# Last heads reordered, the masked bank stored by column, gneg on ScalarE, the output cast in two halves, and w3 split 6:4 over the partition halves by GpSimd transfers

## The chip, the cores and the metric

The kernel runs on one core of one Trainium2 chip. The metric is the device time of one execution in microseconds, and less is better. Three runs of the kernel before give a median of 532.45 us (530.86 to 533.08).

## What is computed

It is one decode step of a transformer block with attention and a gated feed-forward network side by side: four sequences, one new token each, 32 heads of 192 dimensions, a window of 2048 cached positions, everything in bfloat16.

```python
W = min(4096, max(256, Sk // 4))                 # Sk = 8192, so 2048
xn = _layernorm(x)                               # x: (4, 1, 640)
q = (xn @ wq) ...                                # (4, 32, 1, 192)
k, v = k_cache[:, :, Sk-W:], v_cache[:, :, Sk-W:]
p = softmax(q . k * Dh ** -0.5)
attn = (p . v) @ wo                              # wo: (6144, 640)
ffn = (silu(xn @ w1) * (xn @ w3)) @ w2           # F = 1536
out = x + attn + ffn                             # (4, 1, 640)
```

Each head needs 3 MB of K and 3 MB of V (4 sequences x 2048 rows x 192 x 2 bytes each), so 32 heads read 201 MB. wq (7.9 MB), wo (7.9 MB), w1, w3 and w2 (2.0 MB each) make it 223 MB in all.

## The kernel before, in words

The partitions of a K or V tile are (position block, sequence): partition 4p + b holds 64 consecutive positions of sequence b, 24 KB in one piece. One DMA brings the whole tile of a head. There are two K buffers (`KBUFS`) and three V buffers (`VBUFS`).

A head's scores are made in four quarters, called units; unit u is quarter u % 4 of head u // 4, and there are NU = 128 of them.

- `mult(u)` (L231, VectorE) multiplies a quarter of the K tile with the query into `pr`.
- `adder(u)` (L242, TensorE) adds the 192 products down to 32 columns with six matmuls against the identity.
- `reduce_quarter(u)` (L250, VectorE) adds these 32 columns into the scores `sc`.
- The softmax chain of head h: `chain_lmax` (L254, VectorE, maximum per partition), `chain_tr` (L259, a TensorE transpose), `chain_gmax` (L264 the maximum per sequence, L267 `gneg`, that maximum times -1/sqrt(192); both VectorE), `chain_bc` (L272 a matmul that spreads `gneg`, then ScalarE: L275 `negm` and L278 the exponential `ex`), `chain_z` (L286, VectorE, the weights `z`, put into the columns of their sequence).
- `pv(h)` (L295, 24 matmuls) multiplies `z` with the V tile into a PSUM bank, `o_banks[h % 2]`, of 8 groups (j) x 64 columns.
- `pv_diag(h)` (VectorE) masks that bank into `o_m` (L303), then adds it over j into `o_sb` (L306).
- `ge_sum(h)` (L322, TensorE), `ge_tot` (L311), `ge_rec` (L317), `ge_turn` (L326 `og`, L328 `oT`) and `ge_proj` (matmuls through L212) finish a group of four heads: sum over partitions, division by the softmax sum, turn, and product with the group's rows of `wo` into the accumulator `acc`.

The feed-forward part is `ffn_load` (a whole weight as one DMA on SyncE's queue), `ffn_in` (20 matmuls against `xnT`, L345), `ffn_silu`, `ffn_h` (L352, L355), `w2_load` in three pieces and `ffn_out` (matmuls into `acc`). w1, w3 and w2 take turns in one buffer. At the end L447 casts `acc` to `res`, and two DMAs store its halves (L449 on SyncE, L450 on ScalarE).

The order is written out by hand: nothing is moved by a scheduler. `add(slot, phase, fn, ...)` puts a step into a slot (unit u runs in slot u) at a phase, and the loop at the end issues the steps in that order. Each engine works through its own instructions strictly in this order, so an instruction that waits holds all that come after it on its engine. For the last three heads (H-3, H-2, H-1, below called heads 29, 30 and 31) the table `ends` gives slots of their own:

```python
ends = {H - 3: (NU - 3, NU - 2, NU - 1), H - 2: (NU + 2, NU + 3, NU + 4), H - 1: (NU + 6, NU + 7, NU + 7)}
```

The three numbers are the slots of `pv`, `pv_diag` and `ge_sum`. The last V tiles, w2 and the last two groups of `wo` are all issued around slot NU - 6, in the order V29 (second half), V30, V31 (two halves), w2 (eight of twelve columns), wo of groups 6 and 7, w2 (three columns), w2 (one column).

Of the kernel before, what the change touches and what calls it, by code (L numbers as in the profile page):

```python
# [10 lines left out]
FP32 = mybir.dt.float32  # L11
BF16 = mybir.dt.bfloat16
ALU = mybir.AluOpType
ACTF = mybir.ActivationFunctionType
AX = mybir.AxisListType
# [3 lines left out]
def kernel(  # L19
# [20 lines left out]
    nc = tc.nc  # L40
    P = 128
    B, Sq, D = A_x.shape
    _, H, Sk, Dh = A_k_cache.shape
    W = min(4096, max(256, Sk // 4))
    F = B_w1.shape[1]
    KC = D // P
    FC = F // P
    PB = P // B
    NJ = W // PB
    GQ = 4  # L50
    JQ = NJ // GQ
    NK = Dh // DD
    SCALE = float(Dh) ** -0.5
    EPS = 1e-5
    NG = H // HG
    CT = 32
    QW = HG * Dh
    RPP = QW // P
    NU = H * GQ
    N0 = D // 2  # L60
# [3 lines left out]
    JG = CT // B  # L64
    SW = CT * NI
    SR = NS * CT
# [8 lines left out]
    fpool = ctx.enter_context(tc.tile_pool(name="ffn", bufs=1))  # L75
# [3 lines left out]
    const = ctx.enter_context(tc.tile_pool(name="const", bufs=1))  # L79
    ppool = ctx.enter_context(tc.tile_pool(name="pr", bufs=PBUFS))  # L80
    small = ctx.enter_context(tc.tile_pool(name="small", bufs=3))
# [3 lines left out]
    ps_t = ctx.enter_context(tc.tile_pool(name="ps_t", bufs=1, space=MemoryType.PSUM))  # L85
# [27 lines left out]
    x_sb = const.tile([B, D], BF16, name="x_sb")  # L113
# [3 lines left out]
    for k0 in range(0, KC, 2):  # L117
        n = min(2, KC - k0)
        wt = vpool.tile([P, 2, H * Dh], BF16, tag="vt")
        nc.sync.dma_start(out=wt[:, 0:n, :].rearrange("p k n -> p (k n)"),  # L120
                          in_=wq_v[:, k0:k0 + n, :].rearrange("p k n -> p (k n)"))
# [3 lines left out]
    ffn = {}  # L125

    def ffn_load(name, w):
        wt = fpool.tile([P, KC, F], BF16, tag="w", name=name)
        nc.sync.dma_start(out=wt[:].rearrange("p k n -> p (k n)"), in_=w.rearrange("(p kc) n -> p (kc n)", kc=KC))
        ffn[name] = wt  # L130

    ffn_load("w1", B_w1)

    idb = const.tile([P, P], BF16, name="idb")
# [12 lines left out]
    jmask = const.tile([P, NREP], FP32, name="jmask")  # L147
# [8 lines left out]
                            in1=mask_f[:].unsqueeze(1).to_broadcast([P, NS, B]), op=ALU.mult)  # L156
# [18 lines left out]
    xn = const.tile([B, D], BF16, name="xn")  # L175
# [7 lines left out]
    nc.vector.tensor_copy(out=xnT[:], in_=xnT_ps[:].unsqueeze(2).to_broadcast([P, KC, PB, B]))  # L183

    qbc = const.tile([P, H * Dh], BF16, name="qbc")
    for c0 in range(0, NQ, 6):
        qps = [pool.tile([P, QC], FP32, tag=tag, name="qps")
               for pool, tag in ((ps_add, "ps"), (ps_add, "ps"), (ps_o, "o_ps"), (ps_o, "o_ps"), (ps_m, "mt"), (ps_t, "t"))]
        for kc in range(KC):  # L190
            for i, qp in enumerate(qps):
                nc.tensor.matmul(qp[:], lhsT=xnT[:, kc].rearrange("p a b -> p (a b)"),  # L192
                                 rhs=wq_rows[kc][:, (c0 + i) * QC:(c0 + i + 1) * QC],
                                 start=(kc == 0), stop=(kc == KC - 1))
# [8 lines left out]
    o_banks = []  # L203
# [4 lines left out]
    acc = ps_acc.tile([P, N0], FP32, name="acc")  # L208
    nc.vector.memset(acc[:], 0.0)

    def acc_half(i, lhsT, rhs, first=False, last=False):
        nc.tensor.matmul(acc[i * CT:i * CT + B, :], lhsT=lhsT, rhs=rhs[:, i * N0:(i + 1) * N0], start=first, stop=last)  # L212
# [3 lines left out]
            acc_half(i, lhsT, rhs, last=last)  # L216

    po = ps_po.tile([P, SW + 1], FP32, name="po")
    xr = {}

    def x_load():
        xr["t"] = const.tile([B, D], BF16, name="x_res")
        nc.sync.dma_start(out=xr["t"][:], in_=A_x.rearrange("b s d -> (b s) d"))

    def x_add(i):
        acc_half(i, idb[0:B, 0:B], xr["t"], first=True)

    def mult(u):
        h, g = u // GQ, u % GQ
# [32 lines left out]
    def chain_gmax(h):  # L262
        gmax = small.tile([1, B], FP32, tag="gmax")
        nc.vector.tensor_reduce(out=gmax[:], in_=chs[h][1][0:1, 0:P].rearrange("o (p b) -> o b p", b=B),  # L264
                                axis=AX.X, op=ALU.max)
        gneg = small.tile([1, PB, B], FP32, tag="gneg")
        nc.vector.tensor_scalar_mul(out=gneg[:], in0=gmax[:].unsqueeze(1).to_broadcast([1, PB, B]), scalar1=-SCALE)  # L267
        chs[h].append(gneg)

    def chain_bc(h):  # L270
# [28 lines left out]
            vts.pop(h)  # L299

    def pv_diag(h):
        o_m = small.tile([SR, JG, SW], FP32, tag="o_m", bufs=1, name="o_m")
        nc.vector.tensor_tensor(out=o_m[:], in0=o_banks[h % 2][0:SR], in1=jmask[0:SR].unsqueeze(2).to_broadcast([SR, JG, SW]),  # L303
                                op=ALU.mult)
        o_sb = small.tile([SR, SW], FP32, tag="o_sb", bufs=2, name="o_sb")
        nc.vector.tensor_reduce(out=o_sb[:], in_=o_m[:].rearrange("p j c -> p c j"), axis=AX.X, op=ALU.add)  # L306
        o_sbs[h] = o_sb

    def ge_tot(h):
# [27 lines left out]
    FW = F // HG  # L337
# [3 lines left out]
    def ffn_in(name):  # L341
        ffn["ps"] = ps_t.tile([P, FW], FP32, tag="t", name="f_ps")
        for kc in range(KC):
            for w in range(HG):
                nc.tensor.matmul(ffn["ps"][w * CT:(w + 1) * CT, :], lhsT=xnT[:, kc].rearrange("p a b -> p (a b)")[:, 0:CT],  # L345
                                 rhs=ffn[name][:, kc, w * FW:(w + 1) * FW], start=(kc == 0), stop=(kc == KC - 1))

    def ffn_silu():
        nc.scalar.activation(out=sT[:], in_=ffn.pop("ps")[:], func=ACTF.Silu)

# [22 lines left out]
    def add(slot, phase, fn, *args):  # L373
        sched[slot].append((phase, len(sched[slot]), fn, args))

    ends = {H - 3: (NU - 3, NU - 2, NU - 1), H - 2: (NU + 2, NU + 3, NU + 4), H - 1: (NU + 6, NU + 7, NU + 7)}
    for h in range(H):
        u0, ul = h * GQ, h * GQ + GQ - 1  # L380
        if h >= KBUFS:
            add((h - KBUFS + 1) * GQ, 0, load_k, h)
        if h < H - 3:
            add(u0 + 2, 0, load_v, h)
        elif h == H - 3:
            add(u0 + 2, 0, load_v, h, 0, NJ // 2)
            add(NU - 7, 0, load_v, h, NJ // 2, NJ)
        for u in range(u0, ul + 1):
            add(u, 1, mult, u)
            add(u + 1, 2, adder, u)  # L390
            add(u + 1, 8, reduce_quarter, u)
        add(ul + 1, 9, chain_lmax, h)
        add(ul + 2, 3, chain_tr, h)
        add(ul + 2, 4, chain_gmax, h)
        add(ul + 3, 3, chain_bc, h)
        add(ul + 3, 4, chain_z, h)
        add(ul + 4, 5, ge_tot, h)
        if h % HG == HG - 1:
            add(ul + 4, 9, ge_rec, h // HG)
        v, d, m = ends.get(h, (u0 + L, u0 + L + 1, u0 + L + 2))  # L400
        if h < H - 1:
            add(v, 7, pv, h)
        else:
            add(v - 1, 7, pv, h, 0, NJ // 2)
            add(v, 7, pv, h, NJ // 2, NJ)
        add(d, 8, pv_diag, h)
        add(m, 8, ge_sum, h)
        if h % HG == HG - 1:
            add(m + 1, 0, ge_turn, h // HG)
    e = ends[H - 1][2] + 1  # L410
    for hg in range(NG - 2):
        a = ((hg + 1) * HG - 1) * GQ + L + 4
        add(hg * HG * GQ + 8, 0, wo_load, hg)
# [2 lines left out]
    f = FFN_HEAD * GQ  # L416
    add(5, 7, ffn_in, "w1")
    add(5, 9, ffn_silu)
    add(f, 0, ffn_load, "w3", B_w3)
    add(f + 7, 7, ffn_in, "w3")  # L420
    add(f + 7, 9, ffn_h)
    add(8, 0, x_load)
    add(16, 6, x_add, 0)
    add(17, 6, x_add, 1)

# [5 lines left out]
    add(NU - 6, 0, wo_load, NG - 1)  # L432
    add(NU - 6, 0, w2_load, 1)
    add(NU - 6, 0, w2_load, 2)
    add(e - 1, 7, ffn_out, 0)
    add(e - 1, 8, ge_proj, NG - 2, 0, RPP)
    add(e, 6, ge_proj, NG - 1, 0, RPP)
    add(e, 7, ffn_out, 1)
    add(e, 7, ffn_out, 2)
# [4 lines left out]

    NR = CT + B
    res = ppool.tile([NR, N0], BF16, tag="pr", name="res")
    nc.vector.tensor_copy(out=res[:], in_=acc[0:NR, :])  # L447
    out_v = out.rearrange("b s d -> (b s) d")
    nc.sync.dma_start(out=out_v[:, 0:N0], in_=res[0:B, :])  # L449
    nc.scalar.dma_start(out=out_v[:, N0:D], in_=res[CT:NR, :])  # L450
# [30 lines left out]
```

## Time and profile before

| | |
|---|---|
| median of 3 runs | 532.45 us |
| profiled execution, its own time | 533.66 us |
| its span, first to last instruction | 531.9 us |
| TensorE clock granted, mean | 0.89 |
| busy: TensorE, VectorE, ScalarE, GpSimd | 370.4, 392.5, 29.0, 1.1 us |
| HBM read | 222.96 MB, 419 GB/s over the span |

The profiled execution lies 1.2 us above the median, and 1.8 us of it lie outside the span. The times below are us from the start of the span. In a timeline row the first number is the start, the second how long the row lasted, then come engine, line, operation, `out<-in`, shapes and count; the bracket tells how long the engine stood idle before it and what it waited for. A row with a count can hold several instructions with pauses.

### The profile page before, as it was taken

How to read it: one execution, taken by the hardware profiler on the slowest of the kernel's cores; microseconds unless marked ns; L12 is line 12 of the kernel's file. 1: busy time of each engine (PE TensorE's matmuls, PEld its weight loads, DVE VectorE, ACT ScalarE, POOL GpSimd, SP SyncE). 2: the span in 40 equal slices, each digit the busy share in tenths (PEclk: the TensorE clock that was granted, in tenths of full speed). 3: DMA queues.
4: the chain of work that ended last, by engine and by line, in shares of the span. 5: the costliest groups of instructions: out<-in, count | busy, mean ns of one | idle time of the engine just before them, and what ended most of it. 6: DMA issues, size and time to landing. Idle time of an engine off the chain costs nothing.

```text
span 531.9 us, 4826 instructions
## 1 busy us (share of the span) xinstructions
PE 370.4 (70%) x1986; PEld 143.5 (27%) x1987; DVE 392.5 (74%) x498; ACT 29.0 (5%) x110; POOL 1.1 (0%) x8
## 2 busy tenths in 40 slices
PE   2766567677658776468778676567868776876865
PEld 1322222232213322223222222223222322222323
DVE  3178776788948876887858878788768888878853
ACT  2121000000000000000000000000000000000000
POOL 0000000000000000000000000000000000000000
PEclk9989997979978889998977979899787899799777
DMA  8999999999999999999999999999999999999991
GB/s 359 440 425 432 439 427 427 433 439 421 436 429 440 425 434 426 440 425 436 429 434 429 433 430 435 426 436 433 428 433 436 429 433 434 429 434 422 431 420 48
DMA packets 11861, 223.27 MB, mean 420 GB/s; under 512 B 1328, under 2 KB 1472, under 8 KB 2624
## 3 DMA queue, kind: packets, MB, share of 16 engines
q1 hardware_dynamic: 11824, 222.97, 97.7%
q8 instruction: 15, 0.25, 0.2%
q14 instruction: 6, 0.05, 0.0%
q10 hardware_dynamic: 16, 0.01, 0.0%
HBM read 222.96 MB, written 0.01 MB: 419 GB/s over the span
## 4 chain that ended last, share of the span: by engine, by line
DMA 54%; DVE 34%; PE 10%; issue 1%; ACT 0%; SPq 0%
DMA kt<-in_A_k_cache_dram 50%; DVE pr L231 19%; DVE sc L250 5%; PE ps L242 5%; DMA wt<-in_A_wq_dram 4%; DVE o_sb L306 3%; PE o_ps L295 2%; DVE o_m L303 2%; PE qps L192 1%; DVE z L286 1%; DVE gmax L264 1%; DVE gneg L267 1%; PE acc L212 1%; DVE lmax L254 0%; DVE qbc L198 0%
## 5 line engine op out<-in xcount | busy, mean ns | idle before, releaser
L242 PE MATMUL ps<-pr,idb 128*128 128x512 bf16 x768 | 220.7, 431 | 129.0 <-DVE pr L231 128.7
L231 DVE TENSOR_TENSOR pr<-kt,qbc 128x3072 bf16<-128x3072 bf16 x128 | 223.3, 1745 | 88.4 <-DMA kt<-in_A_k_cache_dram 88.4
L242 PEld LDWEIGHTS <-idb 128*128 128x128 bf16 x768 | 78.7, 105 | 240.5 <-issue 182.3
L295 PE MATMUL o_ps<-vt,z 128*32 128x512 bf16 x768 | 100.1, 531 | 1.4 <-DMA vt<-in_A_v_cache_dram 1.4
L250 DVE TENSOR_REDUCE sc<-ps 128x16 f32<-128x512 f32 x128 | 86.8, 678 | 4.5 <-PE ps L242 4.5
L295 PEld LDWEIGHTS <-z 128*32 128x32 bf16 x768 | 32.0, 109 | 56.9 <-issue 55.1
L306 DVE TENSOR_REDUCE o_sb<-o_m 96x64 f32<-96x512 f32 x32 | 32.4, 1012 | 1.1
L275 ACT COPY negm<-mt 128x1 f32<-128x1 f32 x32 | 5.1, 159 | 449.2 <-PE mt L272 449.2
L303 DVE TENSOR_TENSOR o_m<-o_ps,jmask 96x512 f32<-96x512 f32 x32 | 21.5, 673 | 6.4 <-PE o_ps L295 6.4
L192 PE MATMUL qps<-wt,xnT 128*128 128x512 bf16 x59 | 16.1, 429 | 4.8 <-DMA wt<-in_A_wq_dram 4.8
L322 PE MATMUL po<-o_sb,sel_w 96*32 96x64 f32 x64 | 9.7, 234 | 13.2 <-DVE o_sb L306 11.2
L198 DVE CAST qbc<-qps 128x512 bf16<-128x512 f32 x6 | 3.8, 684 | 17.7 <-PE qps L192 17.7
L286 DVE TENSOR_TENSOR z<-ex,mask_b 128x256 bf16<-128x256 bf16 x32 | 13.1, 411 | 4.9 <-ACT ex L278 4.9
L272 PEld LDWEIGHTS mt<-ones_ff,gneg 1*128 1x128 f32 x64 | 9.6, 186 | 14.1 <-DVE o_m L303 10.6
L272 PE MATMUL mt<-ones_ff,gneg 1*128 1x1 f32 x64 | 12.3, 259 | 0.6 <-DVE gneg L267 0.6
L264 DVE TENSOR_REDUCE gmax<-mt 1x4 f32<-1x128 f32 x32 | 8.8, 274 | 4.8 <-PE mt L259 4.8
L278 ACT ACTIVATE ex<-sc,negm 128x64 bf16<-128x64 f32 x32 | 11.1, 348 | 1.0
L259 PE MATMUL mt<-idf,lmax 128*1 128x128 f32 x32 | 9.6, 298 | 1.1 <-DVE lmax L254 1.1
L192 PEld LDWEIGHTS <-xnT 128*128 128x128 bf16 x60 | 6.4, 107 | 14.1 <-issue 8.2
L311 PEld LDWEIGHTS po<-rsum,tot_w 128*32 128x32 f32 x64 | 5.1, 125 | 18.5 <-issue 18.1
L212 PE MATMUL acc<-wo_t,oT 128*4 128x320 bf16 x96 | 9.6, 318 | 0.0
L322 PEld LDWEIGHTS po<-o_sb,sel_w 96*32 96x32 f32 x64 | 4.4, 109 | 17.0 <-DVE o_sb L306 13.8
(54 smaller groups left out, 66.5 us busy)
## 6 DMA issues: line engine op xcount, KB each, us to landing
kt<-in_A_k_cache_dram SPq DMA_DIRECT2D x32, 3072.0 KB, 18.4
vt<-in_A_v_cache_dram SPq DMA_DIRECT2D x30, 3072.0 KB, 25.7
wo_t<-in_A_wo_dram SPq DMA_DIRECT2D x8, 960.0 KB, 19.7
wt<-in_A_wq_dram SPq DMA_DIRECT2D x2, 3072.0 KB, 13.2
vt<-in_A_v_cache_dram SPq DMA_DIRECT2D x4, 1536.0 KB, 21.1
w<-in_B_w_dram SPq DMA_DIRECT2D x2, 1920.0 KB, 30.0
wt<-in_A_wq_dram SPq DMA_DIRECT2D x1, 1536.0 KB, 19.8
w<-in_B_w_dram SPq DMA_DIRECT2D x1, 1280.0 KB, 29.4
```

The lines of the kernel that those rows point to most:

```text
L192: nc.tensor.matmul(qp[:], lhsT=xnT[:, kc].rearrange("p a b -> p (a b)"), rhs=wq_rows[kc][:, (c0 + i) * QC:(c0 + i + 1) * QC], start=(kc == ...
L212: nc.tensor.matmul(acc[i * CT:i * CT + B, :], lhsT=lhsT, rhs=rhs[:, i * N0:(i + 1) * N0], start=first, stop=last)
L231: nc.vector.tensor_tensor(out=pr[:], in0=kts[h][:, g * JQ:(g + 1) * JQ, :], in1=qbc[:, h * Dh:(h + 1) * Dh].unsqueeze(1).to_broadcast([P, ...
L242: nc.tensor.matmul(ps[:], lhsT=idb[:], rhs=pr[:, :, kk * DD:(kk + 1) * DD], start=(kk == 0), stop=(kk == NK - 1))
L250: nc.vector.tensor_reduce(out=scs[h][:, g * JQ:(g + 1) * JQ], in_=pss.pop(u)[:], axis=AX.X, op=ALU.add)
L264: nc.vector.tensor_reduce(out=gmax[:], in_=chs[h][1][0:1, 0:P].rearrange("o (p b) -> o b p", b=B), axis=AX.X, op=ALU.max)
L272: nc.tensor.matmul(mt[:, P:P + 1], lhsT=gneg[:].rearrange("o p b -> o (p b)"), rhs=ones_ff[0:1, 0:1], start=True, stop=True)
L286: nc.vector.tensor_tensor(out=z[:], in0=ex[:].unsqueeze(2).to_broadcast([P, NJ, B]), in1=mask_b[:].unsqueeze(1).to_broadcast([P, NJ, B]), ...
L295: nc.tensor.matmul(o_ps[s * CT:(s + 1) * CT].rearrange("p j c -> p (j c)"), lhsT=z[:, j:j + JG, :].rearrange("p j b -> p (j b)"), rhs=v[:, ...
L303: nc.vector.tensor_tensor(out=o_m[:], in0=o_banks[h % 2][0:SR], in1=jmask[0:SR].unsqueeze(2).to_broadcast([SR, JG, SW]), op=ALU.mult)
L306: nc.vector.tensor_reduce(out=o_sb[:], in_=o_m[:].rearrange("p j c -> p c j"), axis=AX.X, op=ALU.add)
L322: nc.tensor.matmul(po[sl, 0:SW], lhsT=sel_w[0:SR].rearrange("p a b -> p (a b)"), rhs=o_sbs.pop(h)[:], start=True, stop=True)
```

## The change

**Order of the last heads.** The table `ends` goes. `pv` of head 29 is cut into four quarters in slots NU - 5 to NU - 2. `pv` of head 30 is cut into two halves in slots NU + 1 and NU + 2, that of head 31 into halves in NU + 3 and NU + 4, so that it no longer stands behind `ge_sum` of head 30. `pv_diag` of head 29 moves behind the last scores of head 31. The final turn and projection begin in slot NU + 6 instead of NU + 8.

**Masked bank by (column, j).** `o_m` is stored with j innermost. L303's successor reads the PSUM bank with a step of 64 floats and writes without gaps; L306's successor reads without gaps.

**gneg on ScalarE.** The product with -1/sqrt(192) is a ScalarE instruction.

**Cast in halves.** VectorE casts 160 columns of `acc`, ScalarE the other 160. In the built program ScalarE's half waits for VectorE's half (both write the tile `res`), and both stores wait for ScalarE's.

**x** is added into `acc` from `x_sb`, which is in SBUF already; the second load of x (`x_load`) goes.

**w3.** Partitions 0-63 hold six rows of w3 each and partitions 64-127 four, instead of five everywhere. Four DMAs on GpSimd's queue load 32 partitions each: six rows (18 KB in one piece), four rows (12 KB), six, four. They carry no order against SyncE's queue; the first waits for the reads of w1 in the shared buffer. The left operand for the product, `xsT`, is made in the head of the kernel to fit: eight small VectorE copies of `xn` into `xs`, six TensorE transposes, two VectorE copies. `ffn_in_split` runs 24 matmuls instead of 20.

```diff
+    xs = ppool.tile([B, D], BF16, tag="pr", name="xs")
...
+    for p0, d0, kn in SPLIT:
+        for g in range(HP // CT):
+            v = xn[:, d0 + g * CT * kn:d0 + (g + 1) * CT * kn].rearrange("r (b a k) -> r k a b", a=NA, b=NB)
+            nc.vector.tensor_copy(out=xs_m[:, :, p0 // CT + g], in_=v[:, 0:KM])
+            for k in range(KM, kn):
+                nc.vector.tensor_copy(out=xs_x[:, k - KM, g], in_=v[:, k])
...
-        nc.vector.tensor_scalar_mul(out=gneg[:], in0=gmax[:].unsqueeze(1).to_broadcast([1, PB, B]), scalar1=-SCALE)
+        nc.scalar.mul(out=gneg[:], in_=gmax[:].unsqueeze(1).to_broadcast([1, PB, B]), mul=-SCALE)
...
-        o_m = small.tile([SR, JG, SW], FP32, tag="o_m", bufs=1, name="o_m")
+        o_m = small.tile([SR, SW, JG], FP32, tag="o_m", bufs=1, name="o_m")
...
-        nc.vector.tensor_reduce(out=o_sb[:], in_=o_m[:].rearrange("p j c -> p c j"), axis=AX.X, op=ALU.add)
+        nc.vector.tensor_reduce(out=o_sb[:], in_=o_m[:], axis=AX.X, op=ALU.add)
...
+    def ffn_load_split(name, w):
+        wt = fpool.tile([P, KN, F], BF16, tag="w", name=name)
+        nc.gpsimd.inc_swdge_sem([], [], mode="reset_dge_cursor")
+        for g in range(HP // CT):
+            for p0, d0, kn in SPLIT:
+                src = w[d0 + g * CT * kn:d0 + (g + 1) * CT * kn, :].rearrange("(b a k) n -> a b (k n)", a=NA, b=NB)
+                q0 = p0 + g * CT
+                nc.gpsimd.dma_start(out=wt[q0:q0 + CT, 0:kn, :].rearrange("p k n -> p (k n)"), in_=src)
...
-    ends = {H - 3: (NU - 3, NU - 2, NU - 1), H - 2: (NU + 2, NU + 3, NU + 4), H - 1: (NU + 6, NU + 7, NU + 7)}
+    e = NU + 6
+    for g in range(GQ):
+        add(NU - 5 + g, 7, pv, H - 3, g * JQ, (g + 1) * JQ)
+    for g in range(2):
+        add(NU + 1 + g, 7, pv, H - 2, 2 * g * JQ, 2 * (g + 1) * JQ)
+        add(NU + 3 + g, 7, pv, H - 1, 2 * g * JQ, 2 * (g + 1) * JQ)
+    add(NU + 1, 5, pv_diag, H - 3)
+    add(NU + 2, 8, ge_sum, H - 3)
+    add(NU + 3, 8, pv_diag, H - 2)
+    add(NU + 4, 8, ffn_out, 0)
+    add(NU + 4, 8, ge_sum, H - 2)
+    add(NU + 5, 1, pv_diag, H - 1)
+    add(NU + 5, 2, ge_sum, H - 1)
+    add(e, 0, ge_turn, NG - 1)
...
-    nc.vector.tensor_copy(out=res[:], in_=acc[0:NR, :])
+    nc.vector.tensor_copy(out=res[:, 0:N0 // 2], in_=acc[0:NR, 0:N0 // 2])
+    nc.scalar.copy(out=res[:, N0 // 2:N0], in_=acc[0:NR, N0 // 2:N0])
```

In the changed order of the tail TensorE runs: scores of units 125 to 127 with the quarters of `pv(29)` between them, `chain_tr(31)`, first half of `pv(30)`, `chain_bc(31)`, second half of `pv(30)`, `ge_sum(29)`, `ge_tot(31)`, both halves of `pv(31)`, `ffn_out(0)`, `ge_sum(30)`, `ge_sum(31)`, the projections of groups 6 and 7, `ffn_out(1)` and `(2)`. VectorE runs: `mult(127)`, the scores, `chain_lmax(31)`, `chain_gmax(31)`, `pv_diag(29)`, `chain_z(31)`, `pv_diag(30)`, `ge_rec`, `pv_diag(31)`, `ge_turn`, its half of the cast.

More of the change, by code (lines that the diff above doesn't have):

```diff
@@ L127, in ffn_load @@
     def ffn_load(name, w):
-        wt = fpool.tile([P, KC, F], BF16, tag="w", name=name)
-        nc.sync.dma_start(out=wt[:].rearrange("p k n -> p (k n)"), in_=w.rearrange("(p kc) n -> p (kc n)", kc=KC))
+        wt = fpool.tile([P, KC + 1, F], BF16, tag="w", name=name)
+        nc.sync.dma_start(out=wt[:, 0:KC].rearrange("p k n -> p (k n)"), in_=w.rearrange("(p kc) n -> p (kc n)", kc=KC))
         ffn[name] = wt
@@ L183 @@
     nc.vector.tensor_copy(out=xnT[:], in_=xnT_ps[:].unsqueeze(2).to_broadcast([P, KC, PB, B]))
+    KL, KH = KC + 1, KC - 1
+    HP = P // 2
+    NA = 8
+    NB = CT // NA
+    SPLIT = [(0, 0, KL), (HP, HP * KL, KH)]
+    KM = min(KL, KH)
+    PX = 0 if KL > KH else HP
+    KX = KL + KH - 2 * KM
+    xs = ppool.tile([B, D], BF16, tag="pr", name="xs")
+    xs_m = xs[:, 0:KM * P].rearrange("r (k g a b) -> r k g a b", g=P // CT, a=NA, b=NB)
+    xs_x = xs[:, KM * P:D].rearrange("r (k g a b) -> r k g a b", g=HP // CT, a=NA, b=NB)
+    for p0, d0, kn in SPLIT:
[4 more added lines that the diff above has]
+                nc.vector.tensor_copy(out=xs_x[:, k - KM, g], in_=v[:, k])
+    KN = KM + KX
+    xsT = const.tile([P, KN, CT // B, B], BF16, name="xsT")
+    xsT_ps = ps_t.tile([P, KN, B], BF16, tag="t", name="xsT_ps")
+    for k in range(KM):
+        nc.tensor.transpose(out=xsT_ps[:, k, :], in_=xs[:, k * P:(k + 1) * P], identity=idb[0:B, 0:B])
+    for k in range(KM, KN):
+        c0 = KM * P + (k - KM) * HP
+        nc.tensor.transpose(out=xsT_ps[PX:PX + HP, k, :], in_=xs[:, c0:c0 + HP], identity=idb[0:B, 0:B])
+    nc.vector.tensor_copy(out=xsT[:, 0:KM], in_=xsT_ps[:, 0:KM].unsqueeze(2).to_broadcast([P, KM, CT // B, B]))
+    nc.vector.tensor_copy(out=xsT[PX:PX + HP, KM:KN],
+                          in_=xsT_ps[PX:PX + HP, KM:KN].unsqueeze(2).to_broadcast([HP, KX, CT // B, B]))
     qbc = const.tile([P, H * Dh], BF16, name="qbc")
@@ L218 @@
     po = ps_po.tile([P, SW + 1], FP32, name="po")
[L219 to L223, printed above, removed]
     def x_add(i):
-        acc_half(i, idb[0:B, 0:B], xr["t"], first=True)
+        acc_half(i, idb[0:B, 0:B], x_sb, first=True)
     def mult(u):
@@ L301, in pv_diag @@
     def pv_diag(h):
-        o_m = small.tile([SR, JG, SW], FP32, tag="o_m", bufs=1, name="o_m")
-        nc.vector.tensor_tensor(out=o_m[:], in0=o_banks[h % 2][0:SR], in1=jmask[0:SR].unsqueeze(2).to_broadcast([SR, JG, SW]),
-                                op=ALU.mult)
+        o_m = small.tile([SR, SW, JG], FP32, tag="o_m", bufs=1, name="o_m")
+        nc.vector.tensor_tensor(out=o_m[:], in0=o_banks[h % 2][0:SR].rearrange("p j c -> p c j"),
+                                in1=jmask[0:SR].unsqueeze(1).to_broadcast([SR, SW, JG]), op=ALU.mult)
         o_sb = small.tile([SR, SW], FP32, tag="o_sb", bufs=2, name="o_sb")
-        nc.vector.tensor_reduce(out=o_sb[:], in_=o_m[:].rearrange("p j c -> p c j"), axis=AX.X, op=ALU.add)
+        nc.vector.tensor_reduce(out=o_sb[:], in_=o_m[:], axis=AX.X, op=ALU.add)
         o_sbs[h] = o_sb
@@ L346, in ffn_in, with ffn_in_split @@
                                  rhs=ffn[name][:, kc, w * FW:(w + 1) * FW], start=(kc == 0), stop=(kc == KC - 1))
+    def ffn_load_split(name, w):
[6 more added lines that the diff above has]
+                nc.gpsimd.dma_start(out=wt[q0:q0 + CT, 0:kn, :].rearrange("p k n -> p (k n)"), in_=src)
+        ffn[name] = wt
+    def ffn_in_split(name):
+        ffn["ps"] = ps_t.tile([P, FW], FP32, tag="t", name="f_ps")
+        for k in range(KN):
+            q0, q1 = (0, P) if k < KM else (PX, PX + HP)
+            for w in range(HG):
+                nc.tensor.matmul(ffn["ps"][w * CT:(w + 1) * CT, :], lhsT=xsT[q0:q1, k].rearrange("p a b -> p (a b)"),
+                                 rhs=ffn[name][q0:q1, k, w * FW:(w + 1) * FW], start=(k == 0), stop=(k == KN - 1))
     def ffn_silu():
@@ L399 @@
             add(ul + 4, 9, ge_rec, h // HG)
[L400 to L410, printed above, removed]
+        if h < H - 3:
+            add(u0 + L, 7, pv, h)
+            add(u0 + L + 1, 8, pv_diag, h)
+            add(u0 + L + 2, 8, ge_sum, h)
+            if h % HG == HG - 1:
+                add(u0 + L + 3, 0, ge_turn, h // HG)
+    e = NU + 6
[12 more added lines that the diff above has]
+    add(e, 0, ge_turn, NG - 1)
     for hg in range(NG - 2):
@@ L418 @@
     add(5, 9, ffn_silu)
-    add(f, 0, ffn_load, "w3", B_w3)
-    add(f + 7, 7, ffn_in, "w3")
+    add(f, 0, ffn_load_split, "w3", B_w3)
+    add(f + 7, 7, ffn_in_split, "w3")
     add(f + 7, 9, ffn_h)
-    add(8, 0, x_load)
     add(16, 6, x_add, 0)
@@ L434 @@
     add(NU - 6, 0, w2_load, 2)
-    add(e - 1, 7, ffn_out, 0)
-    add(e - 1, 8, ge_proj, NG - 2, 0, RPP)
+    add(e, 5, ge_proj, NG - 2, 0, RPP)
     add(e, 6, ge_proj, NG - 1, 0, RPP)
```

## The prediction

> **What bounds the kernel now.** I read the page first: its slices, queues and chain.
>
> ```profile
> DMA  8999999999999999999999999999999999999991
> ...
> q1 hardware_dynamic: 11824, 222.97, 97.7%
> q8 instruction: 15, 0.25, 0.2%
> q14 instruction: 6, 0.05, 0.0%
> ...
> DMA 54%; DVE 34%; PE 10%; issue 1%; ACT 0%; SPq 0%
> ```
>
> The DMA engines are full from the first slice to the last but one, and almost all of it is one queue, SyncE's. No edit removes bytes worth naming, so until the last transfers nothing that saves engine time shortens the kernel. What is open is how long the kernel goes on after the transfers end. The DMA view of the stretch 512 to 523 us shows that end, in 40 slices of 0.275 us:
>
> ```profile
> DMA  9989999998989999999999886665555534100000
> ```
>
> All engines are busy until about 518.3, about half of them until 521, the last until 521.9 (the last packet in the trace's packet records ends at 521.94). The span ends at 531.9, so 10 us of it are computation alone. The timeline of the tail says which:
>
> ```profile
> 500.63 2.93 PE L295 MATMUL o_ps<-vt,z 128*32 128x512 bf16 x24
> ...
> 505.97 0.43 DVE L286 TENSOR_TENSOR z<-ex,mask_b 128x256 bf16<-128x256 bf16 x1 [2.44 <-ACT ex L278]
> 506.31 0.68 DVE L303 TENSOR_TENSOR o_m<-o_ps,jmask 96x512 f32<-96x512 f32 x1
> ...
> 507.03 1.01 DVE L306 TENSOR_REDUCE o_sb<-o_m 96x64 f32<-96x512 f32 x1
> ...
> 508.55 1.75 DVE L231 TENSOR_TENSOR pr<-kt,qbc 128x3072 bf16<-128x3072 bf16 x1
> ...
> 510.35 2.25 PE L242 MATMUL ps<-pr,idb 128*128 128x512 bf16 x6 [1.96 <-DVE pr L231]
> ...
> 513.73 0.37 PE L259 MATMUL mt<-idf,lmax 128*1 128x128 f32 x1 [1.13 <-DVE lmax L254]
> ...
> 518.88 0.69 DVE L303 TENSOR_TENSOR o_m<-o_ps,jmask 96x512 f32<-96x512 f32 x1 [2.45 <-PE o_ps L295]
> ...
> 520.96 3.62 PE L295 MATMUL o_ps<-vt,z 128*32 128x512 bf16 x22
> ...
> 526.54 1.79 PE L212 MATMUL acc<-wo_t,oT 128*4 128x320 bf16 x22
> ...
> 528.92 0.48 DVE L447 CAST res<-acc 36x320 bf16<-36x320 f32 x1 [1.62 <-PE acc L212]
> 529.43 0.30 SPq L449 DMA_DIRECT2D out_dram<-res  x1
> ```
>
> In the chain of waits the last wait for a transfer ends at 483.93 (`mult(120)`, for K of head 30). From there on it is in-order computation: pv(29) as one block of 2.9 us in front of `chain_bc(30)`, pv_diag(29) in front of `mult(127)`, and pv(31) held until 520.75 by `ge_sum(30)`, which needs `o_sb` at 520.6, though pv(30) was over at 518.9. V31 had landed by 512.3.
>
> **The tail as computation, step by step.** I move the rows along the new order.
> - 483.9 to `mult(124)` at 495.68: VectorE is busy throughout. `gneg` leaves (0.14 between the starts) and `o_sb` shrinks. Its 1.01 us come with steps of 256 bytes; the score reduction of 512 floats (L250) takes 0.68, so I take 0.67 and a saving of 0.34. Together 0.5 earlier.
> - pv(29) in quarters runs where TensorE would idle (0.8 and 1.96 us before the adders of the timeline) or costs 0.9 us each. z(30), 505.97 before, comes at about 504.7. The pv_diag(29) no longer ahead of `mult(127)` saves 1.69. `mult(127)` moves from 508.55 to about 505.5, three earlier.
> - The adder of unit 127 took 2.25 at half clock; at the earlier place the granted clock was full (1.46). `chain_tr(31)` goes from 513.73 to 510.0 or, at half clock, 510.8.
> - Half of pv(30), 1.5 to 1.9, hides the maximum and `gneg`; z(31) stands at 513.2, and pv(30) ends at 514.3. pv(31) then starts with nothing ahead of it: 514.4 instead of 520.75, 6.3 earlier.
> - pv(31) 3.8, then ffn_out(0) 1.5, both `ge_sum` by 520.2; `og`, `oT` 0.6 beside the first 12 projections; all 32 matmuls end 2.5 us later (526.4 to 528.9 before), about 522.5.
>
> `gneg` on ScalarE lies between `negm` (0.16, one element) and the 512-column cast (0.59); I take 0.28, by `ex` with 64 elements (0.35 with its scale). It is covered by half a pv in the tail; without that cover it costs 0.1.
>
> **The masked read.** The only thing against it is that the multiplication now reads PSUM in steps. Three reductions of 128 floats price steps (groups kept apart by shape):
>
> ```profile
> L264 DVE TENSOR_REDUCE gmax<-mt 1x4 f32<-1x128 f32 x32 | 8.8, 274 | 4.8 <-PE mt L259 4.8
> ...
> L142 DVE TENSOR_REDUCE mask_f<-idf 128x4 f32<-128x128 f32 x1 | 0.4, 376 | 0.8 <-POOL idf masks.py:199 0.8
> ...
> L150 DVE TENSOR_REDUCE smask<-idf 128x4 f32<-128x128 f32 x1 | 0.3, 274 | 0.0
> ```
>
> Steps of 16 bytes cost 0.1 us in SBUF (L142 against L150) and nothing in PSUM (L264). So `o_m` stays at 0.67; the other bound is 1.01, as `o_sb` has with steps now. [...]
>
> **The end of the transfers.** 222 MB in SyncE's queue stay full whatever the order. w3 takes the place of itself: GpSimd issues it when w1 has been read (about 45 us, TensorE row L345 at 43.7) and not at 115; K of head 2 lands up to 5 us later, later K as much earlier. GpSimd has nothing else queued. Two costs are new.
> - The split. One engine of a half moves 24.6 KB more or less. 3 MB over 16 engines take 7.27 us between landings, 24.6 KB thus 0.91: the last packet shifts by -0.9 to +0.9. The packet records show why engines end unevenly: each code load (the 16 KB packets of q8) sets one engine back by 1.4 us, and eight engines take them in turn; one other engine takes four 8 KB packets of q14 and ends last, at 521.94. That engine also carried a quarter of the 5 KB reload of x (packets at 71.06, 71.21, 71.23 and 72.19), a load to partitions 0-3. So I take it to serve the half that gets six rows: +0.9, last packet at 522.8. The K of heads 30 and 31 come 0.9 later as well, which takes the first 0.5 back: the computation ends at about 522.9.
> - A second queue. A 16 KB packet between K packets took 0.93 (0.60 at 27 GB/s) and the K packet after it 1.40 for 0.91, so 0.8 are lost; around 8 KB packets 0.3 to 0.5 are. w3 gives each engine eight rows in two transfers. Nothing lost to 8 x 0.8 = 6.6; I take two changes of queue at 0.4, 0.8 in all. Last packet 523.6.
>
> The Trainium skill, "DMA: Bandwidth & Descriptors", sections on SWDGE and HWDGE and on rules for authors, speaks against this: it prefers packets of up to 4096 bytes on GpSimd's path, and says of two transfers to disjoint partition halves not to bother. By 4 KB packets 36 changes per engine at 0.3 would be some 11 us, an estimate from that page's size, and the sum would be 537.
>
> **Hidden edits.** In the head eight copies (142 to 220 ns by the small rows, 1.5 in all) and two more follow `xnT`; the query matmuls wait 1.90 for wq at 10.56 and 1.95 again at 17.80, so 1 us of delay is absorbed; without that cover it costs 1.2. The 28 savings in the loop (0.5 each) lie under VectorE's 88.4 us of waiting for K. The reload of x frees 0.05 of four engines.
>
> **The sum.** The last ffn_out needs the last packet: 523.6, 0.4 to the start (483.5 to 483.93 for K30), 0.3 for two matmuls. The cast: VectorE's half about 0.3, then ScalarE's half 0.3 with a hand-over of 0.1, in series, 0.7 where 0.48 was. Stores 2.4 (529.43 to 531.86). Span 527.4. The computation would allow 526.4, so one us of slack hides it. Against the profiled 531.9 that is 4.5 less: 533.66 - 4.5 = 529.2 for that execution, 1.2 above the median as before: 528.0.
>
> **The rivals.**
> - *The tail stays computation* (0.12): the clock is half throughout, as it was from 510.9 to 524.5. Three adders at 2.7 for 1.46 and a pv more add 4.4; less the slack of 1.0, 3.4: 531.4. For it: clock 0.50 in the windows 512 to 522. Against: full from 500.6 to 510.9.
> - *w3 interleaves row by row* (0.09): 6.6 instead of 0.8, 533.8, hardly different from before.
> - *Slower by the second queue* (0.10): if w3's rows are cut so that more than about eleven changes of 0.8 fall on one engine, the loss eats 4.5 + 2.7 us; twelve to twenty give 537 to 543. For it: every packet of another queue in this trace cost something. Against: those were single packets with code, not a stream with its next packet waiting.
> - *The split relieves the last engines* (0.12): the last one is not in the heavy half. Transfers end at 521.0 + 0.8 and the computation (522.0, as K comes earlier) sets the end: 526.3.
> - *Forecast* (0.57): 526.5 to 529.7.
>
> Faster by over 0.5% (about what a measurement of this kernel can tell from no change; below 529.8): forecast and relief, 0.69. Within: the first two rivals, 0.21. Slower (above 535.1): 0.10. The range 525.0 to 531.6 holds forecast, relief and first rival, the low end with the second queue free of cost.
>
> **What would show it.** Right: pv(31) begins within 0.3 us of the end of pv(30); `o_sb` near 0.67 and `o_m` near 0.67; the last matmuls wait for w2's landing rather than for `oT`; ScalarE's cast starts after VectorE's. Wrong: VectorE waits for K more than 88 us in total while the DMA row keeps its nines, the sign that w3 wasted engine time; w3's landing late enough to hold ffn_in_split near 142; DMA slices that end later than 524; o_m at 1.0 or above.

## The result and the profile after

The changed kernel takes 529.56 us (median of six runs, 528.79 to 529.84), the kernel before 532.77 us in the same set (530.86 to 533.16): a ratio of 0.9944, 95% interval 0.9927 to 0.9961. It is 3.2 us faster. The forecast was 528.0, range 525.0 to 531.6. The profiled execution took 528.79 us with a span of 527.0 us, where the working had 529.2 and 527.4.

The page of the changed kernel, its slices, queues and chain:

```profile
DMA  8999999999999999999999999999999999999994
...
q1 hardware_dynamic: 11672, 221.00, 97.8%
q0 software_dynamic: 320, 1.97, 0.9%
q8 instruction: 15, 0.25, 0.2%
q14 instruction: 6, 0.05, 0.0%
...
DMA 62%; DVE 31%; PE 4%; ACT 1%; issue 1%; SPq 0%
```

The last slice is four tenths busy instead of one, and in the chain TensorE falls from 10% to 4% while DMA rises from 54% to 62%: the kernel ends sooner after its transfers. q0 is GpSimd's queue with w3: the rows of the 128 partitions as 128 packets (64 of 18,432 bytes, 686 ns each, and 64 of 12,288 bytes) and 192 packets of 4 bytes. So the rows of a partition are one packet.

The DMA view of 512 to 527 us, in 40 slices of 0.375 us (each digit is the busy share of the 16 DMA engines in tenths):

```profile
DMA  9999999999899899897866411110000000000000
```

The end looks different: nearly full until 518.7, then down to a tenth (some one or two engines) for 1.5 us. By the packet records the last data packet ends at 522.93; two engines work until 522.28, and the last 0.65 us belong to one engine alone.

The timeline of the tail; brackets give the idle time before a row and what ended it:

```profile
484.98 1.76 DVE L255 TENSOR_TENSOR pr<-kt,qbc 128x3072 bf16<-128x3072 bf16 x1 [3.80 <-DMA kt<-in_A_k_cache_dram]
...
503.88 1.75 DVE L255 TENSOR_TENSOR pr<-kt,qbc 128x3072 bf16<-128x3072 bf16 x1
...
508.26 0.27 PE L283 MATMUL mt<-idf,lmax 128*1 128x128 f32 x1 [1.13 <-DVE lmax L278]
...
511.57 0.52 PE L319 MATMUL o_ps<-vt,z 128*32 128x512 bf16 x2
...
514.05 1.54 PE L319 MATMUL o_ps<-vt,z 128*32 128x512 bf16 x12 [0.83 <-DMA vt<-in_A_v_cache_dram]
...
517.11 0.84 PE L242 MATMUL acc<-w,hT 128*4 128x320 bf16 x10 [1.52 <-DMA w<-in_B_w_dram]
...
519.40 1.76 PE L242 MATMUL acc<-wo_t,oT 128*4 128x320 bf16 x12 [1.04 <-DMA wo_t<-in_A_wo_dram]
521.72 1.44 PE L242 MATMUL acc<-wo_t,oT 128*4 128x320 bf16 x12 [0.55 <-DMA wo_t<-in_A_wo_dram]
522.99 0.71 PE L242 MATMUL acc<-w,hT 128*4 128x320 bf16 x8
523.75 0.32 DVE L495 CAST res<-acc 36x160 bf16<-36x160 f32 x1 [4.69 <-PE acc L242]
524.10 0.28 ACT L496 CAST res<-acc 36x160 bf16<-36x160 f32 x1 [13.13 <-DVE res L495]
```

Before, the last wait for a transfer was at 483.93, for K of head 30. Now TensorE waits for V31, for w2 and for both pieces of `wo`, the last time at 521.72. `pv(31)` starts at 511.57 instead of 520.75. K of head 30 is 1.05 us later (484.98).

### The profile page after: what moved, and what is told of

The parts are those of the page before. It is cut to its first block, busy times and chain, and to the rows that moved or that the text cites. A ratio compares the mean times of both kernels' runs of the same rounds, so it can differ in the third digit from the quotient of the medians.

```text
span 527.0 us, 4868 instructions
## 1 busy us (share of the span) xinstructions
PE 368.4 (70%) x1997; PEld 143.6 (27%) x1997; DVE 375.8 (71%) x476; ACT 39.0 (7%) x143; POOL 3.4 (1%) x12
## 3 DMA queue, kind: packets, MB, share of 16 engines
q0 software_dynamic: 320, 1.97, 0.9%
## 4 chain that ended last, share of the span: by engine, by line
DMA 62%; DVE 31%; PE 4%; ACT 1%; issue 1%; SPq 0%
DMA kt<-in_A_k_cache_dram 52%; DVE pr L255 20%; DMA wo_t<-in_A_wo_dram 6%; DVE sc L274 5%; DMA wt<-in_A_wq_dram 3%; PE qps L222 2%; DVE o_sb L330 2%; DVE o_m L327 2%; PE ps L266 1%; DVE z L310 1%; DVE lmax L278 1%; PE o_ps L319 1%; DVE gmax L288 1%; PE acc L242 0%; DVE oT L352 0%
## 5 line engine op out<-in xcount | busy, mean ns | idle before, releaser
L255 DVE TENSOR_TENSOR pr<-kt,qbc 128x3072 bf16<-128x3072 bf16 x128 | 223.5, 1747 | 107.7 <-DMA kt<-in_A_k_cache_dram 107.7
L319 PE MATMUL o_ps<-vt,z 128*32 128x512 bf16 x768 | 98.5, 520 | 0.8 <-DMA vt<-in_A_v_cache_dram 0.8
L319 PEld LDWEIGHTS <-z 128*32 128x32 bf16 x768 | 30.0, 105 | 54.6 <-issue 53.0
L291 ACT ACTIVATE gneg<-gmax 1x128 f32<-1x128 f32 x32 | 9.8, 308 | 399.9 <-DVE gmax L288 399.9
L330 DVE TENSOR_REDUCE o_sb<-o_m 96x64 f32<-96x512 f32 x32 | 21.8, 682 | 1.1
L242 PE MATMUL acc<-wo_t,oT 128*4 128x320 bf16 x96 | 10.9, 351 | 1.6 <-DMA wo_t<-in_A_wo_dram 1.6
L335 PEld LDWEIGHTS po<-rsum,tot_w 128*32 128x32 f32 x64 | 4.9, 119 | 17.4 <-issue 16.7
```

The lines of the kernel that those rows point to most:

```text
L255: nc.vector.tensor_tensor(out=pr[:], in0=kts[h][:, g * JQ:(g + 1) * JQ, :], in1=qbc[:, h * Dh:(h + 1) * Dh].unsqueeze(1).to_broadcast([P, ...
L319: nc.tensor.matmul(o_ps[s * CT:(s + 1) * CT].rearrange("p j c -> p (j c)"), lhsT=z[:, j:j + JG, :].rearrange("p j b -> p (j b)"), rhs=v[:, ...
L330: nc.vector.tensor_reduce(out=o_sb[:], in_=o_m[:], axis=AX.X, op=ALU.add)
```

## The experiments

Theory A: the order of the last heads is the whole gain; the 6:4 split gives about one microsecond of it back, because the engine that ends last in any case sits in the half with six rows; the small edits are hidden. Rivals: the other edits carry part of the gain; GpSimd's queue and not the split costs the time; the differences are those of the chips.

**e1, the new order alone**, in the kernel before (here and below the edits are cut to the lines that matter):

```diff
-    ends = {H - 3: (NU - 3, NU - 2, NU - 1), H - 2: (NU + 2, NU + 3, NU + 4), H - 1: (NU + 6, NU + 7, NU + 7)}
+    (the slots of the changed kernel, as in its diff)
```

> The kernel before with the new order of the last heads alone; w3 stays five rows everywhere on SyncE's queue, the masked bank, gneg and the cast stay as before, x is reloaded. Theory A (the order of the last heads is the gain, and the 6:4 split costs about 0.9 us because the engine that ends last is in its heavy half): the tail waits for transfers as in the changed kernel, these land 0.9 us earlier, the whole cast saves 0.2, the slower o_sb costs at most 0.4 where it shows: span 526.0 to 526.6, 528.2 to 529.0 us by time. Theory B (the split relieves the engines that end late and is part of the gain): transfers end later than in the changed kernel, span 527.5 to 528.5. Theory C (the shorter masked sum, gneg on ScalarE and the cast carry a good part): span 528 to 530.

Measured: 527.60 us, ratio 0.9911 (0.9890 to 0.9931), below the 528.2 to 529.0 expected. By the medians the order alone gives more than the whole change; its interval lies clear of that of e10 below, the changed kernel again, and just touches that of the first result. The last packet ends at 521.87, as before the change. In the timeline the last waits are for transfers; the last two rows ran at half clock:

```profile
518.34 0.98 PE L212 MATMUL acc<-wo_t,oT 128*4 128x320 bf16 x12 [1.05 <-DMA wo_t<-in_A_wo_dram]
520.63 1.76 PE L212 MATMUL acc<-wo_t,oT 128*4 128x320 bf16 x12 [1.31 <-DMA wo_t<-in_A_wo_dram]
522.18 1.28 PE L212 MATMUL acc<-w,hT 128*4 128x320 bf16 x8
```

**e2, the changed kernel with w3 as before** (five rows everywhere, one transfer on SyncE):

```diff
-    add(f, 0, ffn_load_split, "w3", B_w3)
+    add(f, 0, ffn_load, "w3", B_w3)
...
```

> The changed kernel with w3 as before: five rows on each partition, one transfer on SyncE's queue, no xs. Theory A: the last engine carries 24.6 KB less, everything it holds up lands 0.9 us earlier; the other engines come to 0.6 us before it; span 526.1 against 527.0, the last packet of the records 0.9 earlier. Theory B: the engines relieved by the split come back, last packet about 0.9 later, span 527.9.

Measured: 528.04 us, ratio 0.9919 (0.9900 to 0.9938); last packet 521.75, K of head 30 at 483.87. The late engine is gone from the end:

```profile
521.69 0.71 PE L212 MATMUL acc<-w,hT 128*4 128x320 bf16 x8 [0.17 <-DMA w<-in_B_w_dram]
522.43 0.32 DVE L447 CAST res<-acc 36x160 bf16<-36x160 f32 x1 [4.56 <-PE acc L212]
```

**e3, the split the other way round:**

```diff
-    KL, KH = KC + 1, KC - 1
+    KL, KH = KC - 1, KC + 1
```

> The changed kernel with the split turned round: four rows on partitions 0-63, six on 64-127, the same four GpSimd transfers (the first two exchange sizes). Theory A with its engine count (one late engine in partitions 0-63, eight fairly late ones in 64-127): the one gains 1.8 us, the eight lose 1.8 and become the last, about 0.2 us earlier than the last one in the changed kernel: span 526.7 to 527.0, and in the packet records eight engines end together instead of one alone. If the late engine is in 64-127 instead: its packets end 1.8 us later, span 528.8.

Measured: 528.99 us, ratio 0.9938 (0.9921 to 0.9955), last packet 523.19, where some 522.7 was expected. In the DMA view (512 to 524 us, slices of 0.3 us) not one engine is late but several; by the packet records five work until 522.7:

```profile
DMA  9999989997999999999998767565543433223000
```

So neither direction helps: 6:4 makes one late engine later, 4:6 makes some of the others as late. The prediction called the lucky case "relief"; neither split brings it.

**e4, the kernel before with the w3 split alone:**

```diff
-    add(f, 0, ffn_load, "w3", B_w3)
+    add(f, 0, ffn_load_split, "w3", B_w3)
...
```

> The kernel before with the 6:4 split of w3 by four GpSimd transfers alone. Theory A: K of heads 30 and 31 land 0.6 to 0.9 us later on the last engine, and the tail, all computation from there, ends as much later: span 532.5 to 532.9, time 0.1 to 0.2% above before, too little to tell by time. Theory B: K lands 0.9 earlier, span 531.0. If a second queue costs engine time, the packets end more than 0.9 later.

Measured: 533.91 us, ratio 1.0024 (1.0006 to 1.0041). Alone it costs 1.3 us (0.0024 of 532.95; by the interval 0.3 to 2.2): the old tail hangs on K of head 30, which comes 1.25 later (485.18 instead of 483.93). The last packet came at 523.75, 1.8 later than before and past the 0.9 of the expectation. e9 below, with the same load of w3 and the old order too, has 522.86, so about half of the 1.8 isn't the split's; what it is the runs don't show.

**e5, e2 with the whole cast on VectorE:**

```diff
-    nc.vector.tensor_copy(out=res[:, 0:N0 // 2], in_=acc[0:NR, 0:N0 // 2])
-    nc.scalar.copy(out=res[:, N0 // 2:N0], in_=acc[0:NR, N0 // 2:N0])
+    nc.vector.tensor_copy(out=res[:], in_=acc[0:NR, :])
```

> The changed kernel with w3 as before (five rows, SyncE's queue) and the cast whole again on VectorE. Theory A: the 0.9 us of the split are saved and the serial halves of the cast (0.70 from the first to the second store's issue against 0.51 before) give 0.2 back: span 525.4, 527.5 to 528.3 us by time, better than both kernels. Rival: if the halves are faster than the whole for the stores, 525.8.

Measured: 527.77 us, ratio 0.9924 (0.9905 to 0.9942), no different from e2 within the intervals. In the profile the whole cast has its stores issued 0.51 us after its start (523.56 to 524.07), the halves 0.67 (522.43 to 523.10): the halves lose 0.16. The span was 526.6, not the 525.4 expected, since TensorE's last two rows ran at half clock (1.76 for the 12 projections, as in e1, where e2 had 0.98).

**e6, five rows everywhere, but by four GpSimd transfers:**

```diff
-    KL, KH = KC + 1, KC - 1
+    KL, KH = KC, KC
...
```

> The changed kernel with five rows of w3 on every partition, but by the four GpSimd transfers (15 KB rows, eight per engine): the second queue without the uneven split. If a second queue costs the engines nothing, it ends as e2_w3_even does: span 525.6, last packet at 521.75, both to 0.2. If changes of queue cost what the prediction charged, 0.8 more: 526.4, 522.5.

Measured: 528.11 us, ratio 0.9930 (0.9911 to 0.9949), last packet 522.18. Against e2 the queue costs 0.43 at the last packet (0.10 against e11 below, which is e2 run again). Of the time it costs 0.6 by the ratio of e2 and nothing by that of e11: not told apart from none.

**e7, e5 with one more load of VectorE's code**: 128 writes of one element per partition, spread over units 0 to 111, where VectorE waits for K anyway.

```diff
+        if u < NU - 16:
+            for _ in range(2 if u < 16 else 1):
+                nc.vector.memset(scr[:], 0.0)
...
```

> e5_even_cast with 128 more VectorE instructions, one-column memsets of a scratch column behind the products of units 0 to 111 (two behind the first 16): nothing of the result uses them. They are code alone, some 9 us of VectorE's waiting. Theory A (the engine that ends last does so because it fetches VectorE's code, 8 KB per 128 instructions): one more 8 KB packet on q14, and everything that waits for the last engine 0.8 us later: span 526.2. Rival (it ends last for another reason, or code loads fall on all engines in turn): no more than 0.1.

Measured: 528.37 us, ratio 0.9939 (0.9917 to 0.9961). The intervals of e5 and e7 overlap, so the times alone don't settle it; the trace does. In the two pages the line of the queue with VectorE's code, first e5, then e7:

```profile
q14 instruction: 6, 0.05, 0.0%
```

```profile
q14 instruction: 7, 0.06, 0.0%
```

One 8 KB packet more, and the last packet ends at 522.65 instead of 521.90, K of head 30 starts its product at 484.70 instead of 483.96: 0.75 and 0.74 us later, from 8 KB in 223 MB. That is more than the 0.33 by which the last packets of e2, e5 and e11 differ (521.75 to 522.08). It is one engine that is late: the last but one ends at 521.66 in e5 and at 521.55 in e7.

**e8, the kernel before with one step moved**: `ge_sum(30)` behind `pv(31)`.

```diff
-    ... H - 2: (NU + 2, NU + 3, NU + 4), ...
+    ... H - 2: (NU + 2, NU + 3, NU + 7), ...
```

> The kernel before with one step moved: ge_sum of head 30 behind both halves of pv(31) and ffn_out(0), not ahead of them. Theory A: pv(31) starts at 518.9 where pv(30) ends, not at 520.75, and all after it comes 1.85 earlier: span 530.0. Rival: VectorE's pv_diag(30) or the late z keeps pv(31) where it was: 531.5 or more.

Measured: 529.65 us, ratio 0.9954 (0.9938 to 0.9970): 2.4 us gained by one number, within the intervals as much as the changed kernel gains, and less than e1. The profiled execution (527.75, span 526.0) had TensorE at full clock in its tail (1.00 from 512 to 523 us, 0.50 in the profiled execution of before) and lies 1.9 below the median, so its times aren't compared with those of the kernel before. Its rows show the mechanism, `pv(30)` and `pv(31)` in one piece:

```profile
512.75 1.89 PE L295 MATMUL o_ps<-vt,z 128*32 128x512 bf16 x15
514.44 3.94 PE L295 MATMUL o_ps<-vt,z 128*32 128x512 bf16 x33
```

**e9, the changed kernel with the old order; e10, the changed kernel again; e11, e2 again**, the three on one chip:

```diff
-    (the slots of the changed kernel)
+    ends = {H - 3: (NU - 3, NU - 2, NU - 1), H - 2: (NU + 2, NU + 3, NU + 4), H - 1: (NU + 6, NU + 7, NU + 7)}
...
```

> The changed kernel with the old order of the last heads; the 6:4 split, the masked bank, gneg and the cast in halves stay. Theory (the order is the gain; the small edits are hidden only because the new tail waits for transfers): here the tail is computation again, so the small edits show. o_sb loses 0.33 us at each pv_diag that stands in the path (in front of mult(127), in front of ge_sum(30), and the last one before og), gneg about 0.1 at mt, the cast adds 0.2. From e4_w3_only (533.9, with the split and the old tail) that is 533.9 - 1.0 - 0.1 + 0.2 = 533.0, span about 531. Rival 1 (the small edits cost or give nothing even in a tail of computation): 534.0. Rival 2 (the order is not the gain, the other edits carry it): 530 or below.

> The changed kernel unaltered, beside e11 on the same chip, so that the price of the split is read within one set of runs. Theory (the split costs 0.9 at the last packet and up to 0.5 more by lateness of every tile): 0.9 to 1.4 us above e11. Rival (the difference of 1.5 between the first runs and e2 was a difference between chips): equal to e11 within 0.4.

> The changed kernel with w3 loaded as before (five rows everywhere, one transfer on SyncE), as e2. Theory: last packet 21.7 to 21.9 us past 500, and 0.9 to 1.4 us less than e10. Rival (no price of the split): equal to e10 within 0.4.

Measured: e9 532.02 us, ratio 0.9996 (0.9983 to 1.0009); e10 529.44, 0.9953 (0.9941 to 0.9966); e11 528.40, 0.9936 (0.9923 to 0.9948). Everything but the order, taken together, gives nothing; the order takes 2.6 us off it. The price of the split with its queue, on one chip, is 529.44 - 528.40 = 1.04 us, and the last packets tell the same: 523.10 against 522.08, and K of head 30 at 485.14 against 484.14. So it was not a difference between chips.

Between e4 (1.0024) and e9 (0.9996) stand the small edits under the old order: 1.5 us gained, where 0.9 was expected; the two intervals leave 1.1 us either way. Under the new order (e1 against e2, e5 and e11) they gain nothing that the intervals show. That fits what VectorE saves counting only where VectorE is in the path.

## Why the prediction was right, and where it was off

**What bounds the kernel: right.** "10 us of it are computation alone", which the new order moves beside the transfers. e1 has all of the gain (by the medians some 2 us more), e9 without the order none.

**The computation of the tail: right in direction; one term was too small, and the clock hid it.** The list, before its shift by late K, had z(30) at 504.7, `mult(127)` at 505.5, `chain_tr(31)` at 510.0 and `pv(31)` at 514.4. They came at 502.93, 503.88, 508.26 and 511.57, though K of head 30 was 1.05 late. `mult(124)` began at 496.15; the text's 0.5 saved and 0.9 lost give 496.08. The surplus arises behind it, at `chain_bc(30)`, and has two parts, which e9 separates: it has the old order, and in its profile the granted clock was 1.00 from 495 to 500.5 us, as in that of the changed kernel, where before it was 0.50. Before, e9 and the changed kernel; the last row of each is `chain_bc(30)`:

```profile
495.21 5.28 PE L242 MATMUL ps<-pr,idb 128*128 128x512 bf16 x12 [0.82 <-DVE pr L231]
...
504.89 0.38 PE L272 MATMUL mt<-ones_ff,gneg 1*128 1x1 f32 x2
```

```profile
497.87 1.45 PE L266 MATMUL ps<-pr,idb 128*128 128x512 bf16 x6 [0.81 <-DVE pr L255]
...
499.36 2.90 PE L319 MATMUL o_ps<-vt,z 128*32 128x512 bf16 x24
...
503.60 0.38 PE L296 MATMUL mt<-ones_ff,gneg 1*128 1x1 f32 x2
```

```profile
497.95 1.46 PE L266 MATMUL ps<-pr,idb 128*128 128x512 bf16 x6
...
499.52 0.86 PE L319 MATMUL o_ps<-vt,z 128*32 128x512 bf16 x6
...
501.85 0.38 PE L296 MATMUL mt<-ones_ff,gneg 1*128 1x1 f32 x2
```

Counted from `mult(124)` (495.68, 496.07 and 496.15) that is 9.21, 7.53 and 5.70 us (7.55 in e4 and e8, where pv(29) is one block too). So of 3.5 us, 1.8 are the order and 1.7 are the clock, by which the adders of units 123 and 124 took 2.6 instead of 1.45 each. The mis-sized term is pv(29) in quarters, credited 0.8 (the 1.3 at z(30) less the 0.5 saved ahead of it): the block of 2.9 us had stood whole in front of `chain_bc(30)`, and now one quarter of 0.86 stands between `chain_tr(30)` and the adder.

The same holds further on: `pv(31)` came 9.2 earlier than before, where 6.3 were forecast, but 6.8 earlier than in e9 (518.37), which has the small edits and K of head 30 as late (484.91); and in e9 the adder of unit 127 ran at half clock (2.7 us). Most of the 2.9 beyond the forecast is thus the clock of one profiled execution. The surplus bought nothing: `pv(31)`'s second half waits 0.83 for V31, ffn_out(0) 1.52 for w2.

Three figures of the prediction are slightly off, without consequence: 8 x 0.8 is 6.4, not 6.6; 522.9 with 0.7 and 2.4 behind it is 526.0, not 526.4; the last packet of V31 ended at 512.69, not by 512.3.

**The masked read and gneg: right.** Groups kept apart by shape:

```profile
L327 DVE TENSOR_TENSOR o_m<-o_ps,jmask 96x512 f32<-96x512 f32 x32 | 21.4, 670 | 2.7 <-PE o_ps L319 2.7
L330 DVE TENSOR_REDUCE o_sb<-o_m 96x64 f32<-96x512 f32 x32 | 21.8, 682 | 1.1
L291 ACT ACTIVATE gneg<-gmax 1x128 f32<-1x128 f32 x32 | 9.8, 308 | 399.9 <-DVE gmax L288 399.9
```

VectorE's reading of PSUM in steps of 256 bytes costs nothing (670 ns; 673 without steps), and the reduction without steps takes 682 instead of 1012. The Trainium skill ("SBUF — State Buffer", DMA port swizzle) says that access patterns with gaps in PSUM slow matmuls; these VectorE reads were not slowed by them. gneg took 0.308 for an estimated 0.28.

**The split: right, with its sign and size.** "+0.9, last packet at 522.8": the last packet was at 522.93. The split alone is the changed kernel less e6: 0.75 at the last packet, 0.92 in e10. e10 less e11, 1.02 at the last packet and 1.04 in time, has the second queue with it. The guess from four small packets, which half the last engine serves, held: with six rows in that half the one late engine ends later (522.93 against 522.18 in e6), and with six rows in the other half (e3) five end late together. e7 shows why there is one late engine at all.

**The second queue: mis-sized.** The sum had "two changes of queue at 0.4, 0.8 in all". By e6 it is 0.1 to 0.4 at the last packet. The row that it was taken from, single packets of code between K packets, doesn't describe a stream of big rows. The Trainium skill ("DMA: Bandwidth & Descriptors", rules for authors) says not to bother with two transfers to disjoint partition halves. The advice proved sound: four even transfers gained nothing (e6), and uneven halves cost most of the microsecond. The 4 KB packets of the prediction's estimate did not occur: the rows went as whole 12 and 18 KB packets.

**The end of the sum: right in total, with errors that partly cancel.** In the profiled execution "The last ffn_out needs the last packet" isn't quite how it ended: the last wait is the projections' for `wo` of group 7 at 521.72, they took 1.44 at a clock of 0.50 up to 522.7 (0.98 at full clock in e10), and w2's eight matmuls followed without a wait at 522.99, 0.06 after the last packet. In e10, at full clock, the wait is for w2 as foreseen (in e2 too, by the row shown there):

```profile
523.05 0.71 PE L242 MATMUL acc<-w,hT 128*4 128x320 bf16 x8 [0.19 <-DMA w<-in_B_w_dram]
```

From the last packet to the cast 0.82 (0.7 foreseen), cast with hand-over to the store 0.66 (0.7), from there to the end of the span 2.6 (2.4). 527.0 stands against 527.4: 0.7 less than foreseen at the last packet, mostly the queue's, and 0.3 more behind it.

**From the profiled execution to the median: this is what missed.** The text took the profiled execution to lie 1.2 above the median after the change too. It lay 0.8 below. Had the two been set equal, the median would have come out at 529.2. The profiled execution of before was slow where the tail was slow: granted clock 0.50 in the whole stretch of 512 to 523 us. e9, a tail of computation too, had it at 1.00 there and lay 1.6 below its median. The windows of the kernel before and then of e9; behind the stretch and its length stand PE busy (and matmuls), clock, DMA share and GB/s:

```profile
512.00:523.00 11.00, 7.34 (x50) 0.50 0.73 306
```

```profile
512.00:523.00 11.00, 7.61 (x75) 1.00 0.75 314
```

With a tail bound by transfers the scatter gets smaller: twelve runs of the changed kernel lie between 528.71 and 530.05, the runs of the kernel before in the same two sets between 530.85 and 533.19. That fits an offset which belonged to the old tail and could not be carried over; one profiled execution of each kernel suggests it and doesn't show it. It also means that the gain depends on the clock: at 1.00 in the tail the spans are 528.7 in e9 and 527.1 in e10, 1.6 apart, where the medians of the two are 2.6 apart.

**The signs.** Those of being right held, with the exception told above for w2. One of being wrong came up and was badly chosen: VectorE's wait for K rose from 88.4 to 107.7 us with all slices of the DMA row full, which the text called a sign that w3 wasted engine time. VectorE's busy time fell by 16.7 us (392.5 to 375.8), which accounts for nearly all of these 19.3: savings under a full DMA row turn into waiting.

**The rivals.** That the tail stays computation fell with the waits above; row by row interleaving and the slow second queue fell with e6; relief fell with the last packet (523.10 in e10 against 522.08 in e11) and, for the other direction, with e3.

**What is better.** e1 and e5 (527.60 and 527.77) have lower medians than both kernels. Against e10, e1's interval is clear and e5's just touches; between e1 and e5 the intervals don't decide. The simplest is e1, the new order alone.

## What to carry to other kernels

Look for the last wait for a transfer in the chain: what runs after it is worth taking apart, and there a block of work in front of a short chain of dependent steps counts in full. Before a gain is put down to an edit, compare the granted clock of the same stretch in both profiles: here half of the 3.5 us at one step was the clock. Savings on an engine that waits for transfers become waiting; the same savings in a tail of computation become time. Where transfers are full on all engines, bytes must stay even between them. And a profiled execution's distance from the median need not outlast a change of the tail.

## What was not expected of the hardware

- Code loads set DMA engines back. Of the six 8 KB packets of q14, four come at even distances, and e7's 128 more VectorE instructions made them five. As far as packets can be followed from end to start, these lie on one engine (the other two on others). Each sets it back by about 0.8 us (0.75 in e7), though the packet itself takes 0.31: the K or V packet behind it, 24,576 bytes, takes 1.44 instead of 0.91. The 16 KB packets of q8, taken here for TensorE's code, go to eight other engines in turn and cost 1.4 us each. So the number of VectorE's instructions makes one engine the last to finish.
- A second queue beside a full first one, with 15 KB packets (e6), cost at most 0.4 us at the last packet (1.97 MB in q0 in the changed kernel).
- The granted clock in the last 15 us differs between executions of one kernel: from 519.3 to 522.7 it was 0.50 in the first profile of the changed kernel and 1.00 in e10. The ten to twelve runs each of e4, e8 and e9, with tails of computation, spread over 2.9 to 3.7 us, the four to six runs of each kernel with the new order over 0.7 to 1.4. That the clock makes this difference fits the profiles but isn't shown run by run; what sets it in a given execution the runs don't show.
